# A random-feature attention and two expert layers on one core: wider VectorE and ScalarE steps, another share for GpSimd, token forms earlier

## The chip, the cores and the metric

The kernel runs on one core of one Trainium2 chip. What counts is device time in microseconds. The kernel before takes 965.62 us, the median of three runs (962.77 to 966.36).

## The reference

Three layers follow one another. The first is linear attention with random features, the others are two dense layers with a hidden width of 2048. Inputs are q, k, v of 4 x 8 x 576 x 64, 128 random features, and the weights, which come as 64-bit floats.

```python
def phi(x):                                  # random features, scaled by D ** -0.25
    proj = einsum('bhsd,md->bhsm', x, omega)
    h = proj - sum(x * x, -1) / 2
    return exp(h - max(h)) / sqrt(m)
q_p, k_p = phi(q_s), phi(k_s)
kv, z = einsum('bhsm,bhsd->bhmd', k_p, v), sum(k_p, axis=2)
x = (q_p @ kv) / (q_p @ z + 1e-6)            # 2304 tokens x 512
h = x @ w_in;   x = (h * cos(h)) @ w_out     # 512 -> 2048 -> 512
h = x @ w2_in;  x = (h * clip(h + 3, 0, 6) / 6) @ w2_out
```

## The kernel before, in words

**A planner writes the order.** Each piece of work is a task with a key (a due time), the engines that may do it with a duration for each, the tasks that it comes after, and the buffers that it takes and uses (`Plan.add`). `Plan.order` plays all tasks through: an engine that is free takes the ready task with the lowest key, if a slot of its buffer ring is free. Keys are formulas of tuned constants plus a tuned offset for each kind (`BIAS`). The result is the order of instructions on every engine. Where a task may go to VectorE or GpSimd, `SLOW` gives its durations and `ENGS` the choice, for each phase: 0 is the first two weight pairs and the first stop, 1 the rest of the first dense layer, 2 the second.

**Attention.** 18 chunks of 128 tokens, first the keys, then the queries (some of the queries among the keys). For each: a load, a projection, squares, a minimum on VectorE, the exponential on ScalarE, and matmuls. A query chunk ends in a transpose (line 626) and a copy into `xx`, the activations that stay in SBUF.

**Two splits.** Weights arrive as pairs of 32-bit words. `weight` makes 32-bit floats from them in one ScalarE step (line 698) and four VectorE steps (clamp line 702, shift 706, sign 712, low word 718), 512 columns at a time. Matmul operands are then split in a high part (rounded, `rnd`, line 377) and a low part (`sub`, line 384), and each product is three matmuls: high by high, low by high, high by low.

**First dense layer, four of 16 blocks of 128 hidden columns.** `pair_slot` computes them in the plain way (lines 827 and 853) beside the queries; this part I call the plain stage.

**The other 12 blocks, and all 16 of the second layer.** They go in pairs by a scheme of Strassen's kind: seven products (line 1062) replace eight. `pair_forms` makes seven weight forms of a pair (sums and differences, split), `forms` makes seven token forms `xf` of 768 tokens (b11, b21, b22, t1 to t4; four of them sums, line 1026) and stores them in DRAM (line 1041), from where later sweeps load them (line 994). A tour of 21 stops goes over seven sweeps of two pairs and three token ranges; each stop has two groups (`quad`), 42 groups in all. In a group the seven products go into four PSUM banks, which are seeded from one another by ScalarE (line 1075). VectorE adds for two of the four blocks (lines 1097 and 1100), and the nonlinear function follows for each block by itself: for cos lines 1127 or 1129, 1132, 1136 to 1141, 1145 or 1147, for the second layer lines 1114 and 1117; then the split into `g2`. One stop later `units` multiplies these by the second weight matrix (line 1186) into one of two banks, and line 1207 adds the bank to `xx`.

**Buffers.** `RINGS` names slots of shared memory. Weights arrive in `ws` and `ws2` and are converted in `wt` (three slots). `R2` lies on the memory of attention's buffers and opens when the last chunk is done (`open`).

All DMAs are issued from one queue, SP's, in the planner's order. Gaps of TensorE that the planner expects in attention are filled with small matmuls (lines 1252 and 1261).

Of the kernel before, what the change touches and what calls it, by code (L numbers as in the profile page):

```python
# [41 lines left out]
T_K = 5.034  # L42
T_Q = 18.765
T_S = 5.44
W_K0 = 32.072
W_KD = 0.874
W_AFTER = [3, 9]
W_F = [(-155.9, 30), (-90.9, 30)]
NS = 384
NP = 2 * NS  # L50
SWEEP = 2
L_PAIRS = [(NF - NG) // 2, NF // 2]
# [10 lines left out]
def stacked(space, at, *sizes):  # L63
    made = {}
    for ring, width, n in sizes:
# [9 lines left out]
    **stacked(F1, XX, ("ws", 1024, 3), ("wt", 512, 3), ("wk", 512, 3), ("yp", 512, 3)),  # L75
# [21 lines left out]
BIAS = {"sqnk": -64.1, "rd": 40.4, "kvs": 1.3, "g": 103.5, "xh": 39.3, "r1": 35.1, "gl": 52.5, "kv": -38.6, "b1q": 28.2, "h": 30.0, "in": -85.5, "W11": 34.6, "yp": -349.2, "xTk": -14.9, "y": 31.8, "vk": -12.4, "gh": 328.6, "tp": -94.6, "pjk": -188.3, "natk": -162.5, "xt": -131.2, "ek": -384.4, "sqq": 94.1, "xn": -159.4, "b1k": -156.9, "mxk": -366.5, "num": -75.3, "xl": 40.2, "sqnq": 187.5, "qt": -39.1, "xx": -230.5, "xTq": -5.7, "wk": -42.0, "natq": -168.8, "sn": -5.8, "W10": 92.9, "mxq": -40.0, "pjq": -166.6, "eq": -64.2, "sqk": -242.2, "out": 45.6, "ps": -16.5, "P00": 15.3, "P01": 37.0, "P10": 104.7, "P11": -4.2, "P20": -192.8, "P21": -393.2, "b2k": 16.5, "b2q": -82.4, "ba0": 35.7, "ba1": 81.9, "ba2": 86.8, "bb0": -448.0, "bb1": 142.2, "bb2": 367.5, "bc0": 84.4, "bc1": -169.0, "bc2": -161.9, "bd0": -180.6, "bd1": -359.0, "bd2": -149.6, "be0": -200.1, "be1": 38.4, "be2": -35.0, "c120": -131.9, "c121": 126.3, "c122": 262.4, "c220": -170.7, "c221": 104.1, "c222": -1.5, "consts": 162.6, "ev20": -93.6, "ev21": 76.5, "ev22": 130.6, "g20": -83.4, "g21": -262.0, "g22": 220.0, "gg0": 221.0, "gg1": -217.3, "gg2": -33.0, "gl20": -133.0, "gl21": 166.0, "gl22": 339.0, "ident": 199.0, "nq0": 283.2, "nq1": -8.6, "nr0": -36.2, "nr1": -65.2, "nt0": 119.2, "nt1": -3.2, "om": 115.1, "omr": -243.4, "open": -425.0, "pr0": -275.8, "pr1": -17.8, "pr2": -14.3, "pr3": 14.6, "psk": 147.5, "psq": -199.4, "rec": -225.8, "s50": 215.0, "s51": 54.7, "s52": -370.4, "sp0": -53.6, "sp1": -1.6, "sp2": -25.1, "st0": 54.8, "st1": -19.4, "st2": 54.1, "sum0": 103.2, "sum1": 208.3, "sum2": 101.9, "ta0": 37.4, "ta1": -8.1, "ta2": -7.3, "table": 15.7, "tb0": 37.6, "tb1": -7.2, "tb2": -1.3, "warm": 324.8, "wf0": 95.1, "wf1": 394.2, "wf2": -44.6, "wfh0": -163.2, "wfh1": -81.9, "wfh2": 218.8, "wfl0": 7.6, "wfl1": -44.7, "wfl2": -221.9, "wk20": -156.7, "wk21": -94.1, "wk22": -423.0, "wo0": -59.4, "wo1": -163.1, "wo2": 86.0, "woh0": -465.7, "woh1": -431.0, "woh2": -193.4, "wol0": 245.8, "wol1": 5.3, "wol2": -181.0, "xf0": 27.0, "xf1": 199.3, "xf2": 171.0, "xfl0": 210.5, "xfl1": 0.5, "xfl2": 234.6, "xst0": -135.9, "xst1": -249.1, "xst2": -136.0, "y20": -27.0, "y21": 31.9, "y22": 101.5, "yp21": -296.7, "yst": 9.8}  # L97
# [9 lines left out]
SLOW = {"sum": {"v": 0.42, "p": 0.89}, "wfla": {"v": 0.68, "p": 1.36}, "wflb": {"v": 0.42, "p": 0.89}, "wflc": {"v": 1.22, "p": 2.35}, "wol": {"v": 0.68, "p": 1.36},  # L107
        "gl2": {"v": 0.58, "p": 1.13}, "xfl": {"v": 0.95, "p": 1.83}, "ta": {"v": 0.95, "p": 1.83}, "xf": {"a": 0.84, "p": 1.3}}
ENGS = {"sum0": "v", "sum1": "v", "sum2": "p", "wfla0": "p", "wfla1": "p", "wfla2": "v", "wflb0": "p", "wflb1": "v", "wflb2": "v", "wflc0": "p", "wflc1": "p", "wflc2": "p", "wol0": "p", "wol1": "p", "wol2": "v", "gl20": "p", "gl21": "p", "gl22": "p", "xfl0b11": "v", "xfl0b21": "p", "xfl0b22": "v", "xfl1b11": "p", "xfl1b21": "p", "xfl1b22": "p", "xfl2b11": "p", "xfl2b21": "p", "xfl2b22": "v", "u0b": "a", "u1b": "a", "u0d": "a", "u1d": "a", "u0r": "v", "u1r": "v", "u0q": "v", "u1q": "v", "xfl0t1": "v", "xfl0t2": "v", "xfl0t3": "v", "xfl0t4": "p", "xfl1t1": "v", "xfl1t2": "v", "xfl1t3": "v", "xfl1t4": "v", "xfl2t1": "p", "xfl2t2": "p", "xfl2t3": "p", "xfl2t4": "p", "ta0t1": "p", "ta0t2": "v", "ta0t3": "p", "ta0t4": "v", "ta1t1": "p", "ta1t2": "v", "ta1t3": "p", "ta1t4": "v", "ta2t1": "v", "ta2t2": "v", "ta2t3": "v", "ta2t4": "p", "xf0": "ap", "xf1": "ap", "xf2": "a"}
# [50 lines left out]
class Plan:  # L160
# [9 lines left out]
    def order(self):  # L170
# [68 lines left out]
        while len(done) < len(tasks):  # L239
# [6 lines left out]
            while again:  # L246
                again = False
                for e in engines:
# [3 lines left out]
                    while pool[e]:  # L252
# [4 lines left out]
                        c = can(t, now)  # L257
# [19 lines left out]
                    free[e] = end  # L277
                    wake(end)
# [24 lines left out]
def attention_moe_moe2_kernel(  # L303
# [8 lines left out]
    eye: bass.AP,  # L312
    w1: bass.AP,
# [8 lines left out]
    halfpi, three, magic = (consts_[:, i:i + 1] for i in range(3))  # L322
# [45 lines left out]
    def wh(f):  # L368
        return held(plan.slot["wh", 1, f, 0], [128, 1024])

    def wl(f):
        sp, lo, hi = plan.slot["wh", 1, f, 0]
        return held((sp, lo + 1024, hi), [128, 1024])
# [25 lines left out]
    def consts(e):  # L399
        nc.gpsimd.memset(halfpi, HALFPI)  # L400
        nc.scalar.activation(out=junk, in_=halfpi, func=ACTF.Exp)
        nc.gpsimd.memset(three, 3.0)
        nc.gpsimd.memset(magic, MAGIC)
# [280 lines left out]
    def weight(src, m, f, hf, j=None):  # L684
        W = (m, f, hf)
        k = W_K0 + W_KD * (2 * f + hf) if j is None else w_key(j) + 6.0 * (f % 2) + 12.0 * hf
        cols = slice(512 * hf, 512 * hf + 512)

        def load(e):
            t = tile_of(("ws",) + W, [128, 1024], U32)  # L690
            nc.sync.dma_start(out=t, in_=src[f, :, 1024 * hf:1024 * hf + 1024])

        gate = [] if j is None else [("ba", 3 * j - 5 - j % 2)] if j >= SWEEP else [("in", W_AFTER[j], 3)]
        add(("ws",) + W, k - 8, {"d": 1.5}, load, gate + ([last_w[0]] if last_w[0] and j is None else []), alloc="ws" if j is None else "ws2", soft=[last_w[0]] if last_w[0] and j is not None else [])

        def mag(e):
            w = tile_of(("wt",) + W, [128, 512])
            nc.scalar.activation(out=w, in_=word(W, 1).bitcast(F32), func=ACTF.Abs)

        def clamp(e):  # L700
            w = buf[("wt",) + W]
            (nc.gpsimd if e == "p" else nc.vector).tensor_scalar(out=w, in0=w, scalar1=F64_HUGE, scalar2=F64_TINY, op0=ALU.min, op1=ALU.max)  # L702

        def shift(e):
            u = buf[("wt",) + W].bitcast(U32)
# [4 lines left out]
        def sign(e):  # L710
            u = buf[("wt",) + W].bitcast(U32)
# [4 lines left out]
        def low(e):  # L716
            u = buf[("wt",) + W].bitcast(U32)
# [4 lines left out]
        S_, T_ = ("ws",) + W, ("wt",) + W  # L722
# [608 lines left out]
```

## Time and profile before

| | |
|---|---|
| Median of three runs | 965.62 us |
| The profiled execution | 964.89 us, its span 963.0 us |
| TensorE busy (matmul) | 920.2 us, 96% |
| VectorE busy | 697.6 us, 72% |
| ScalarE busy | 562.5 us, 58% |
| GpSimd busy | 425.7 us, 44% |
| Mean granted clock of TensorE | 0.987 |

Attention runs from 0 to 220 us and the plain stage from 84 to 274 us. The groups of the first layer begin at 230 us, the last product ends at 930 us, the last matmul at 959 us. A busy share counts the time in which an engine has an instruction in work. A time of VectorE or GpSimd holds whatever the instruction waits for once it has begun.

### The profile page before, as it was taken

The page shows a single profiled execution, that of the slowest core. Times are in us where ns is not written, and L with a number is a line of the kernel's source. Part 1 is how long each engine was busy: PE and PEld are TensorE (multiplying, and loading weights), DVE is VectorE, ACT ScalarE, POOL GpSimd, SP SyncE. Part 2 cuts the span into 40 slices and gives each one's busy share as a digit, 9 for nine tenths or more (in the row PEclk, how much of TensorE's full clock was granted, in tenths as well). Part 3 has the DMA queues.
Part 4 walks back from the last instruction along what each step waited for, and adds up shares of the span by engine and source line. Part 5 has one row for each costly group of instructions (what it writes and reads, how often), then busy time and mean ns, then how long its engine had stood idle before and what let it go on. Part 6 is the DMA issues. An engine that isn't in the chain of part 4 may idle for free. (4 is left out here: it accounts for less than half of the span.)

```text
span 963.0 us, 18009 instructions
## 1 busy us (share of the span) xinstructions
PE 920.2 (96%) x6974; PEld 893.2 (93%) x6974; DVE 697.6 (72%) x1172; ACT 562.5 (58%) x1211; POOL 425.7 (44%) x342
## 2 busy tenths in 40 slices
PE   9999999999888999999998799999998999899998
PEld 8888999999888989989998699889998999899998
DVE  5896888767899996996799978763596459734332
ACT  7888787875655746646555666565463445334330
POOL 3431434215876443542455785761454135522230
PEclk9999999999999999999999999999999999999999
DMA  8754343213656539723561572354471257023512
GB/s 265 243 192 147 112 136 111 88 54 123 241 197 240 190 112 346 265 67 114 209 216 75 189 283 104 129 204 158 182 251 44 103 205 265 18 98 150 213 66 99
DMA packets 48134, 156.57 MB, mean 163 GB/s; under 512 B 4912, under 2 KB 16176, under 8 KB 48048
## 3 DMA queue, kind: packets, MB, share of 16 engines
q1 hardware_dynamic: 48048, 155.41, 45.6%
q8 instruction: 55, 0.90, 0.4%
q14 instruction: 31, 0.25, 0.1%
HBM read 112.93 MB, written 42.47 MB: 161 GB/s over the span
## 5 line engine op out<-in xcount | busy, mean ns | idle before, releaser
L384 POOL TENSOR_TENSOR R<-F,R 128x384 fp32r<-128x384 f32 (+3 forms) x254 | 336.9, 1345 | 420.9 <-ACT R L377 301.4
L377 ACT ACTIVATE R<-F 128x384 fp32r<-128x384 f32 (+4 forms) x306 | 173.9, 603 | 124.5 <-PE b L1186 40.6
L1186 PE MATMUL b<-R 128*128 128x384 f32 x1116 | 232.4, 338 | 10.3 <-DVE F L1207 10.1
L1186 PEld LDWEIGHTS b<-R 128*128 128x128 f32 x1116 | 198.7, 190 | 12.9 <-DVE F L1207 12.9
L1186 PE MATMUL b<-R,R 128*128 128x384 f32 x900 | 195.8, 339 | 8.0 <-DVE F L1207 7.9
L1062 PE MATMUL b<-R,R 128*128 128x384 f32 x978 | 187.7, 338 | 15.3 <-ACT b L1075 11.9
L1062 PEld LDWEIGHTS b<-R,R 128*128 128x128 f32 x978 | 171.8, 190 | 19.1 <-ACT b L1075 14.8
L1186 PEld LDWEIGHTS b<-R,R 128*128 128x128 f32 x900 | 161.6, 191 | 10.0 <-DVE F L1207 9.9
L1062 PE MATMUL b<-R 128*128 128x384 f32 x786 | 151.1, 339 | 1.5 <-ACT b L1075 1.5
L1207 DVE SCALAR_TENSOR_TENSOR F<-b,F 128x384 f32<-128x384 f32 x144 | 78.9, 552 | 93.5 <-PE b L1186 91.7
L1062 PEld LDWEIGHTS b<-R 128*128 128x128 f32 x786 | 140.0, 191 | 2.2 <-ACT b L1075 2.2
L1075 ACT ACTIVATE b<-b 128x384 f32<-128x384 f32 x126 | 60.0, 477 | 74.6 <-PE b L1062 73.2
L533 ACT ACTIVATE F<-b,F 128x128 f32<-128x128 f32 x288 | 81.6, 398 | 14.1 <-DVE F L518 12.8
L384 DVE TENSOR_TENSOR R<-F,R 128x512 fp32r<-128x512 f32 (+2 forms) x70 | 77.7, 1115 | 10.4 <-ACT R L377 7.9
L377 ACT ACTIVATE F<-b 128x512 f32<-128x512 f32 (+2 forms) x104 | 54.6, 540 | 30.4 <-PE b L1062 16.2
L507 DVE TENSOR_REDUCE F<-b 128x4 f32<-128x512 f32 x72 | 48.2, 684 | 22.2 <-PE b L490 14.1
L718 DVE SCALAR_TENSOR_TENSOR F<-F 128x512 uint32<-128x512 uint32 x64 | 62.7, 980 | 0.2
L853 PE MATMUL b<-R 128*128 128x256 f32 x432 | 60.0, 289 | 1.1 <-ACT F L869 1.1
L827 PE MATMUL b<-R 128*128 128x256 f32 x432 | 57.9, 286 | 0.3 <-DVE F L514 0.3
L712 DVE SCALAR_TENSOR_TENSOR F<-F 128x512 uint32<-128x512 uint32 x64 | 56.7, 886 | 0.6
L853 PEld LDWEIGHTS b<-R 128*128 128x128 f32 x432 | 54.9, 192 | 2.4 <-ACT F L869 1.3
L827 PEld LDWEIGHTS b<-R 128*128 128x128 f32 x432 | 53.8, 191 | 1.0 <-issue 0.5
(72 smaller groups left out, 1044.3 us busy)
## 6 DMA issues: line engine op xcount, KB each, us to landing
R<-xd SPq DMA_DIRECT2D x70, 768.0 KB, 7.0
F<-w SPq DMA_DIRECT2D x64, 512.0 KB, 4.4
xd<-R SPq DMA_DIRECT2D x42, 768.0 KB, 3.4
F<-vn SPq DMA_DIRECT2D x18, 260.0 KB, 4.5
F<-qT SPq DMA_DIRECT2D x18, 256.0 KB, 2.7
yy<-F SPq DMA_DIRECT2D x18, 256.0 KB, 2.3
F<-yy SPq DMA_DIRECT2D x24, 192.0 KB, 2.6
yT<-F SPq DMA_DIRECT2D x12, 384.0 KB, 2.4
```

The source lines that it names most:

```text
L377: nc.scalar.activation(out=o, in_=i, func=ACTF.Copy)
L384: (nc.gpsimd if e == "p" else nc.vector).tensor_tensor(out=o, in0=a, in1=b, op=ALU.subtract)
L507: nc.vector.tensor_reduce(out=buf[MX][:, o:o + 4], in_=pj, axis=AX.X, op=ALU.min)
L533: nc.scalar.activation(out=p[:, o], in_=pj[:, o], func=ACTF.Exp, scale=-1.0, bias=mx[:, b:b + 1])
L712: nc.vector.scalar_tensor_tensor(out=u, in0=word(W, 1), scalar=SIGN_HI, in1=u, op0=ALU.bitwise_and, op1=ALU.bitwise_or)
L718: nc.vector.scalar_tensor_tensor(out=u, in0=word(W, 0), scalar=29, in1=u, op0=ALU.logical_shift_right, op1=ALU.bitwise_or)
L827: nc.tensor.matmul(out=o, lhsT=w[:, 128 * kc:128 * kc + 128], rhs=v, start=(kc == 0 and j == 0), stop=(kc == KC - 1 and j == 2), skip_grou ...
L853: nc.tensor.matmul(out=y, lhsT=w[:, o], rhs=v, start=(first and fi == 0 and j == 0 and ec % 2 == 0), stop=(last and fi == 1 and j == 2 and ...
L1062: nc.tensor.matmul(out=o, lhsT=a, rhs=v, start=first and kc == 0 and q == 0, stop=kc == 1 and q == 2, skip_group_check=True)
L1075: nc.scalar.activation(out=buf[to][:, 0:NS], in_=buf[frm][:, 0:NS], func=ACTF.Copy)
L1186: nc.tensor.matmul(out=o, lhsT=a, rhs=v, start=q == 0, stop=q == 6 * SWEEP - 1)
L1207: nc.vector.scalar_tensor_tensor(out=o, in0=y, scalar=r, in1=o if s else buf[YP], op0=ALU.mult, op1=ALU.add)
```

## The change

- **Weights.** One staging slot of 2048 words (`ws2`), one conversion slot of 1024 columns (`wt`); `ws` has two slots of 2048. `weight` works on 1024 columns. The host packs each pair so that the front half holds the four blocks of the first matrix in the order in which forms need them, the rear half the second matrix. Splits of 512 and 256 columns become one of 768, two of 512 one of 1024.
- **Nonlinear function.** The two off-diagonal blocks lie side by side in `hs` and are done in one step of 768 columns (block "r"), also in their split; the diagonal ones ("b", "d") as before. Rings `g3` and `wk3` hold the wide tiles.
- **GpSimd.** `ENGS` chooses anew. The planner lets a GpSimd task and a VectorE task that reads only SBUF (`shares`) not overlap: both take a lock. The lock is the planner's; the kernel has no wait for it.
- **ScalarE.** Constants pi/2, 3 and the rounding constant are given as numbers, not as a column of a tile.
- **First stop's token forms.** With `AHEAD = 1` the seven forms of the first 768 tokens are made through one slot (`xe`) and two for sums (`te`) from key 150 on, stored in DRAM, and loaded when `R2` opens.
- **Order.** New keys and offsets throughout. A weight pair of each layer's second sweep waits for the last token form of that layer (`gate`). The seeds of a group come after the last seed of the group before. `SEED`, a list for another way to start output banks, is empty.

```diff
+AHEAD = 1
+AHEAD_AT = [150.0, 190.0, 220.0]
+AHEAD_BY = 4.0
+SEED = [[], [], [], [], [], [], []]
...
-    **stacked(F1, XX, ("ws", 1024, 3), ("wt", 512, 3), ("wk", 512, 3), ("yp", 512, 3)),
+    **stacked(F1, XX, ("ws", 2048, 2), ("wt", 1024, 1), ("wk", 512, 3), ("yp", 512, 2)),
...
-    "g2": spread(R1, 16384, 768, 8) + spread(R2, 13312, 768, 4),
-    "ws2": spread(F1, XX, 1024, 2),
-    "ta": spread(F1, XX + 1024, 768, 2),
+    "g2": spread(R1, 16384, 768, 4) + spread(R2, 13312, 768, 2),
+    "g3": spread(R1, 19456, 1536, 2) + spread(R2, 14848, 1536, 1),
+    "xe": spread(R1, 14336, 1536, 1),
+    "te": spread(F1, XX + 3072, 768, 1) + spread(F1, XX + 2048, 768, 1),
+    "ws2": spread(F1, XX, 2048, 1),
+    "ta": spread(F1, XX, 768, 2),
...
+SHARED = ("clamp", "shift", "sign", "low", "wl", "xl", "gl", "wfl", "wol", "st", "sum", "ta", "tb", "xfl", "gl2")
...
+            if (e == "p" or e == "v" and t.shares) and lock[0] > now:
+                return lock[0]
...
+                    if e == "p" or e == "v" and t.shares:
+                        lock[0] = end
...
-            w = tile_of(("wt",) + W, [128, 512])
-            nc.scalar.activation(out=w, in_=word(W, 1).bitcast(F32), func=ACTF.Abs)
+            nc.scalar.activation(out=tile_of(T_, [128, 1024]), in_=word(W, 1).bitcast(F32), func=ACTF.Abs)
...
+        gate = [("ba", 3 * j - 5 - j % 2)] if j >= SWEEP else [("in", W_AFTER[j], 3)]
+        for m in range(2):
+            if j == m * L_PAIRS[0] + SWEEP + 1:
+                gate.append(("tb", m, NT // NP - 1, "t4"))
...
-            nc.scalar.activation(out=buf[WK], in_=buf[WK], func=ACTF.Sin, scale=-TURN, bias=halfpi)
+            nc.scalar.activation(out=buf[WK], in_=buf[WK], func=ACTF.Sin, scale=-TURN, bias=HALFPI)
...
-        made = part("a", 0, 512, lambda: buf[f0], [f0], [low[0]], alloc="wf")
-        made += part("b", 512, 256, lambda: buf[f1][:, 256:512], [f1], [low[1]])
+        made = split("a", WF, FORM_HI, 0, 768, lambda: buf[T0][:, 0:768], [T0], [("low", j, 0)], 0, "wf")
...
+            ahead = s == 0 and p < AHEAD
+            if s not in heads or ahead:
...
+                    add(X, k + 2.0 * i - 14, {"d": 2.4}, load, [("xst", m, p, i)] + (["open"] if ahead else []), alloc="xf", soft=behind(i))
...
-            for r, c, h, done, dk in ((0, 0, A, c11, 5.2), (1, 1, ("c22", n), ("c22", n), 10.5), (0, 1, ("s5", n), ("c12", n), 12.1), (1, 0, Dk, c21, 13.8)):
+            for x, h, done, dk in (("b", A, c11, 5.2), ("r", HS, ("c12", n), 12.1), ("d", Dk, c21, 13.8)):
+                N = NP if x == "r" else NS
...
-                        nc.scalar.activation(out=tile_of(WK, [128, NS]), in_=buf[h][:, 0:NS], func=ACTF.Relu, bias=three)
+                        nc.scalar.activation(out=tile_of(WK, [128, N]), in_=hv(), func=ACTF.Relu, bias=3.0)
```

## Rows read from the trace of the kernel before

**Rows 1.** The page: busy us of each engine, share of the span, instructions.
```profile
PE 920.2 (96%) x6974; PEld 893.2 (93%) x6974; DVE 697.6 (72%) x1172; ACT 562.5 (58%) x1211; POOL 425.7 (44%) x342
```

**Rows 2.** Stretches: length, busy us of PE, PEld, DVE, ACT, POOL, clock, DMA.
```profile
150.00:205.00 55.00, 55.00 (x616) 51.79 (x617) 43.93 (x105) 45.01 (x100) 17.32 (x15) 1.00 0.30 97
...
230.00:330.00 100.00, 89.58 (x525) 87.44 (x525) 91.07 (x122) 63.19 (x124) 71.27 (x48) 0.95 0.60 218
330.00:430.00 100.00, 95.29 (x543) 93.69 (x542) 89.68 (x159) 58.43 (x114) 44.48 (x35) 1.00 0.58 200
...
500.00:555.00 55.00, 45.34 (x241) 43.74 (x240) 50.71 (x64) 29.85 (x58) 36.17 (x27) 0.95 0.42 158
555.00:650.00 95.00, 90.75 (x513) 89.02 (x512) 70.99 (x93) 57.93 (x113) 65.99 (x47) 0.99 0.48 176
650.00:830.00 180.00, 172.99 (x972) 171.07 (x971) 119.50 (x182) 87.51 (x173) 74.41 (x64) 0.98 0.45 164
830.00:959.00 129.00, 128.88 (x744) 128.56 (x742) 46.62 (x85) 41.66 (x84) 28.40 (x28) 1.00 0.31 114
```

**Rows 3.** Waits of TensorE: for whom, us in total, times, longest us.
```profile
PE b L1186 <- DVE F L1207: 18.1, 11, 3.1
PE b L1062 <- ACT b L1075: 13.5, 12, 3.4
```

**Rows 4.** Timeline 699 to 728 us: start, us, what, idle before.
```profile
705.78 0.41 DVE L702 TENSOR_SCALAR F<-F 128x512 f32<-128x512 f32 x1
...
708.59 0.68 DVE L718 SCALAR_TENSOR_TENSOR F<-F 128x512 uint32<-128x512 uint32 x1
...
720.85 1.22 DVE L712 SCALAR_TENSOR_TENSOR F<-F 128x512 uint32<-128x512 uint32 x1
721.49 3.99 POOL L384 TENSOR_TENSOR R<-F,R 128x384 fp32r<-128x384 f32 x3
...
723.14 1.48 DVE L718 SCALAR_TENSOR_TENSOR F<-F 128x512 uint32<-128x512 uint32 x1
...
725.61 0.79 PE L1186 MATMUL b<-R,R 128*128 128x384 f32 x3 [3.06 <-DVE F L1207]
```

**Rows 5.** Timeline 214 to 245 us.
```profile
219.25 0.60 PE L626 MATMUL b<-F 128*128 128x128 f32 x4
...
226.43 0.94 DVE L384 TENSOR_TENSOR R<-F,R 128x768 fp32r<-128x768 f32 x1
...
230.43 1.21 PE L1062 MATMUL b<-R 128*128 128x384 f32 x6
```

**Rows 6.** VectorE by line and shape: count, busy us, mean ns, idle before.
```profile
L718 DVE SCALAR_TENSOR_TENSOR F<-F 128x512 uint32<-128x512 uint32 x64 | 62.7, 980 | 0.2
L712 DVE SCALAR_TENSOR_TENSOR F<-F 128x512 uint32<-128x512 uint32 x64 | 56.7, 886 | 0.6
...
L702 DVE TENSOR_SCALAR F<-F 128x512 f32<-128x512 f32 x64 | 40.9, 638 | 10.4 <-ACT F L698 10.3
...
L1129 DVE TENSOR_SCALAR F<-F 128x384 f32<-128x384 f32 x36 | 28.0, 778 | 1.2
...
L1147 DVE SCALAR_TENSOR_TENSOR F<-F 128x384 f32<-128x384 f32 x36 | 25.7, 720 | 1.3 <-ACT F L1138 1.3
```

**Rows 7.** GpSimd by line and shape.
```profile
L384 POOL TENSOR_TENSOR R<-F,R 128x384 fp32r<-128x384 f32 x168 | 188.4, 1139 | 296.8 <-ACT R L377 196.4 <-PE b L1186 50.0 <-DVE F L1207 24.6
```

**Rows 8.** ScalarE by line and shape.
```profile
L1114 ACT ACTIVATE F<-F,consts 128x384 f32<-128x384 f32 x48 | 29.6, 616 | 19.3 <-DVE F L1097 11.1 <-DVE F L1100 6.1 <-POOL R L384 1.1
...
L1136 ACT ACTIVATE F<-F 128x384 f32<-128x384 f32 x36 | 18.6, 517 | 9.1 <-DVE F L1132 8.7
```

**Rows 9.** DMA issues: count, KB each, median us to landing.
```profile
R<-xd SPq DMA_DIRECT2D x70, 768.0 KB, 7.0
F<-w SPq DMA_DIRECT2D x64, 512.0 KB, 4.4
```

**Rows 10.** TensorE's fillers by line and shape.
```profile
L1252 PE MATMUL b<-F 128*128 128x128 f32 x46 | 7.7, 293 | 0.0
```

More of the change, by code (lines that the diff above doesn't have):

```diff
@@ L256, in order @@
                             continue
-                        c = can(t, now)
+                        c = can(t, now, e)
                         if c == 0.0 and any(
@@ L321, in attention_moe_moe2_kernel @@
     consts_ = const.tile([128, 16], F32, name="consts")
-    halfpi, three, magic = (consts_[:, i:i + 1] for i in range(3))
+    one = consts_[:, 0:1]
     space = {
@@ L399, in consts @@
     def consts(e):
[L400 to L403, printed above, removed]
+        nc.gpsimd.memset(one, 1.0)
+        nc.scalar.activation(out=junk, in_=one, func=ACTF.Exp)
         nc.gpsimd.memset(half, 0.5 * SCALE * SCALE)
@@ L988, in forms @@
             m = int(s >= heads[1])
-            if s not in heads:
+            ahead = s == 0 and p < AHEAD
+            if s not in heads or ahead:
                 for i, x in enumerate(names):
@@ L994, in load @@
                         nc.sync.dma_start(out=tile_of(X, [128, 2 * NP]).bitcast(F32), in_=xd[n_p * m + p, i])
-                    add(X, k + 2.0 * i - 14, {"d": 2.4}, load, [("xst", m, p, i)], alloc="xf", soft=behind(i))
-                return
-            gate = [("ba", n - 2)] if n else []
+                    add(X, k + 2.0 * i - 14, {"d": 2.4}, load, [("xst", m, p, i)] + (["open"] if ahead else []), alloc="xf", soft=behind(i))
+                if not ahead:
+                    return
+            gate = [("ba", n - 2)] if n and not ahead else []
             ready = [("ev2", s - 1, p, u) for u in range(8)] if m else [("xx", c) for c in range(NP // 128 * p, NP // 128 * (p + 1))]
@@ L1065, in product @@
                 add(name, k + 2.1 * ORDER.index(i), {"t": 1.04}, fn,
-                    forms_made + ([("xfl", int(s >= heads[1]), p, x)] if s in heads else []) + list(after), alloc=alloc, use=[X, ("wf", j)] + ([] if alloc else [bank_of]) + list(use))
+                    forms_made + ([("xfl", int(s >= heads[1]), p, x)] if s in heads and (s or p >= AHEAD) else []) + list(after), alloc=alloc, use=[X, ("wf", j)] + ([] if alloc else [bank_of]) + list(use))
                 return name
@@ L1077, in seed @@
                 add(to, k + dk - 10, {"a": 0.5}, fn, after, alloc=ring, use=[frm])
[L1079 removed]
+            first = ["open"] if n == 0 else [("ba", n - 1)] + ([("bd", 0)] if n == 1 else [("bd", n - 2)] if n else []) + ([("y", N_A - 1, 2)] if n == 2 else [])
             product(0, A, True, first, ring)
[L1081 removed]
+            seed(Bk, A, 1.1, [A] + ([("bd", n - 1)] if n else [f"pr{i}" for i in range(4)]))
             product(4, E, True, [A], ring)
+            HS = ("hs", n)
             def s5(e):
[L1085 to L1087 removed]
+                rnd(e, tile_of(HS, [128, NP])[:, 0:NS], buf[E][:, 0:NS])
+            add(HS, k + 3.2 - 8, {"a": 0.5}, s5, [("c22", n - 2)] if n > 1 else [], alloc="hs", use=[E])
             c11 = product(1, A, False, [Bk, E])
@@ L1134, in sine, with rest @@
+                    def rest(e, hv=hv, WK=WK):
+                        nc.vector.scalar_tensor_tensor(out=buf[WK], in0=buf[WK], scalar=MAGIC, in1=hv(), op0=ALU.subtract, op1=ALU.subtract)
                     def sine(e, WK=WK, on_act=on_act):
```

351 lines of the change are left out of this document (174 added, 177 removed).

## The prediction

> **What bounds the kernel now.** I read the busy shares first: TensorE is busy for 920.2 of 963.0 us and VectorE for 697.6 [rows 1]. So TensorE is the engine to feed, but a mean over the whole span hides where it starves, and the table by stretches is the view to read next [rows 2]. There the reader is to compare TensorE's busy time with the length of each stretch, and VectorE's beside it. From 830 to 959 us TensorE works without a break: 744 matmuls in 128.88 us, 0.173 us each, and this pace is a floor, because the change leaves every matmul of the three computing stages as it is. Elsewhere TensorE is idle for 10.42 us (230 to 330), 4.71 (330 to 430), 9.66 (500 to 555), 4.25 (555 to 650) and 7.01 (650 to 830): 36.05 us together. In the three worst of these stretches VectorE is busy for 91%, 90% and 92%; from 830 to 959, where nothing is lost, for 36%. The granted clock is the second loss. Short spells at 1.2 GHz, all of them in or right behind stretches in which TensorE stood still, make the column read 0.95, 0.95, 0.99 and 0.98: 5.0 + 2.75 + 0.95 + 3.6 = 12.3 us of full-speed time. So 36.05 + 12.3 = 48.4 us lie open behind 230 us, and 964.89 - 48.4 = 916 is what would be left with none of it.
>
> The waits of TensorE say who is late [rows 3]: 18.1 us for line 1207 (VectorE moves a finished output bank into the residual; there are only two such banks) and 13.5 us for line 1075 (ScalarE seeds the next product bank). Neither step is long. They are late because their engine's queue is behind. The timeline around the longest one shows how [rows 4]: GpSimd runs three subtractions in a row for 3.99 us, and beside them VectorE's line 712 takes 1.22 us and line 718 1.48 us, where line 718 takes 0.68 alone. The output bank's move starts behind these and TensorE waits 3.06 us. VectorE lost about 0.54 + 0.80 us on the two steps shown, some 45% of that stall, to running beside GpSimd.
>
> **The change, part by part.** All sums are against the profiled execution: 964.89 us, a span of 963.0 and 1.9 around it; the median of the runs, 965.62, is 0.7 above it.
>
> *Weights twice as wide.* The 64 half-width conversions become 32. Their four VectorE rows sum to 62.7 + 56.7 + 40.9 + 40.7 = 201.0 us [rows 6] (the last, line 706, is of line 702's kind). Alone, line 718 took 0.68 us for 512 columns and line 702 0.41 [rows 4], and a subtraction 0.94 for 768 [rows 5]. So 256 columns of the first kind cost 0.26, their fixed part is 0.16, and 384, 256 and 1024 columns cost 0.55, 0.42 and 1.20. No row shows a step at 1024 columns: twice a half-width step is the upper end, the fixed part less the lower. Clamp and shift then take 0.66 to 0.82; I take 0.8, nearest to the row. A set of 1.20, 1.20, 0.8 and 0.8 costs 4.0, and 32 sets 128 us: 73 less. If the wide steps collide as the narrow ones do now, 201.0 less the fixed parts (64 x 4 halved, 0.16 each: 20) is 181, only 20 less.
>
> *The two off-diagonal blocks in one step of 768 columns.* In the first layer lines 1129, 1132 and 1147 take 28.0 + 25.2 + 25.7 = 78.9 us in 36 triples [rows 6] (line 1132, between the two shown, is of line 1147's kind); 18 triples of three steps of at most 0.94 are 51 us: 28 less. Against it, the wide tile starts only when both blocks are there, so one block's answer is later by some 2 us. That is covered: the tiles are read one stop of the tour later, two groups of seven products on.
>
> *Work moved from GpSimd to VectorE.* Of the low halves of the activations (168 on GpSimd, 1139 ns each [rows 7]), 4 + 48 steps of 384 columns and 16 + 24 of 768 go to VectorE: 52 x 0.55 + 40 x 0.94 = 66 us. Weight forms go from 12 + 24 steps of 256 and 512 columns to 6 of 768 and 24 of 1024, 13 us more; the sums of weights from 24 to 56, 13 us; the token forms add 10 steps of 768, 9 us. Together 101 us more on VectorE, and GpSimd keeps about 190 of its 425.7 us, counted in the same way. VectorE's total is then 697.6 - 73 - 28 + 101 = 698. The four weight rows hold 201.0 - 64 x 2.18 = 61 us of lengthening beside GpSimd; if as much of that stays as GpSimd keeps, 45%, 27 us come back, and the rows that I left as they are give up about as much. I take 690, between 650 and 740. So VectorE does not become light. What changes is that a step of 0.7 us stays at 0.7 more often when an output bank waits behind it.
>
> The lengthening stands in the rows. The Trainium skill (SBUF — State Buffer, section "Who interferes with whom") gives a rule for it: a VectorE instruction with two SBUF inputs and a GpSimd one that reads SBUF exclude each other for the whole instruction. By it a wide step shuts GpSimd out for longer, and each collision costs the later of the two the rest of the other; in the rows GpSimd's three steps took 3.99 us where three means are 3.42, so both sides pay, as the rule has it. What that would make of the time is the rival "only the head" below.
>
> *Constants as immediates on ScalarE.* Line 1114 with a constant tile takes 616 ns, line 1136, the same shape without it, 517 [rows 8]. Of 186 such instructions 144 remain after merging: 14 us of ScalarE, or none if an immediate is fetched like a tile. ScalarE is never the engine that is full behind 230 us, so I count it at nothing by itself; were it the last link of each of 42 groups it would be 4 us.
>
> *First pass's token forms beside the queries.* This takes seven roundings, seven subtractions and four sums out of the stretch from 221 to about 245 us and puts them beside the queries: at most 7 x 2 x 0.517 = 7 us on ScalarE [rows 8], 3 x 0.94 = 3 on VectorE and, at twice a 384-column step's 1139 ns at the most [rows 7], 8 x 2.28 = 18 on GpSimd. Between 150 and 205 us GpSimd is busy for 17.32 of 55 and VectorE for 43.93 [rows 2], so they fit. If that cover fails, TensorE is late there by up to 10 us, ScalarE's 7 and VectorE's 3 taken whole. SP issues seven more loads of 768 KB and these wait for the last attention chunk; each lands 7.0 us after its issue [rows 9]. TensorE's last transpose of a chunk began at 219.25 us and the first product at 230.43 [rows 5], so there is room for one landing, and the later loads follow while the other products and the last blocks of the plain stage run. In the stretch 230 to 330 VectorE loses some 6 of its 91.07 us and GpSimd about as much.
>
> *Shared and fewer buffers, one more order.* One 2048-word staging slot for weights where there were two of half the size, one conversion slot where there were three; the token sums lie on the staging slot. Where a conversion is on time this costs nothing; its price if not is the rival below. The seeds of a group now come behind the last seed of the group before; both are ScalarE's and in that order already: nothing.
>
> *Keys and biases of the planner.* Every queue is written in another order. No row prices that. In the attention stage fillers of 7.7 us stand for gaps that the old plan expected [rows 10]; these may go (-8) or grow (+8), and I take zero.
>
> **The sum.** 230 to 330: 10.4 + 5.0 lost; the forms leave and GpSimd's runs shorten; I keep 5: -10. 330 to 430: 4.7 to 2.5: -2. 500 to 555: there the second layer's token forms and weights still meet, and VectorE gets more of them; 12.4 to 7: -5.5. 555 to 830: 11.3 + 4.5 lost; 45% as in the stall of rows 4: -7. Together -24.5: 964.9 - 24.5 = 940.
>
> **Rivals.** *Everything goes that is open.* All VectorE bursts dissolve and with them the low clock: 916, or, with a few us left, 922. For it: 830 to 959 shows the pace without loss. Against it: VectorE stays at 690.
>
> *Only the head gains.* GpSimd's rest still meets the wide steps (181 us for the weights in place of 128), so the low halves that it keeps and the output banks behind VectorE's longer steps are late as now, or the immediates are fetched like tiles. Then only the token forms help: -10, 955.
>
> *The stalls are dealt anew.* VectorE near 700 us means that first-layer groups need about as much VectorE as before (85 to 90% of 330 to 430), and another order puts the same waits elsewhere: 963.
>
> *Slower: one conversion slot.* Front and rear half of a pair now go through one slot in series. Front: ScalarE 1, four steps 4.0, rounding and subtraction of 768 columns 1.8, four sums 1.7, rounding and subtraction of 1024 columns 2.2: 10.7. Rear: 1 + 4.0 + 2.2 = 7.2. A load of 512 KB lands in 4.4 us [rows 9], one of 1 MB in about 8.5, of which some 4 lie beside the splitting of the half before: 2 x 4. With handovers that is 27 us a pair, and a pair is needed every three groups, 3 x 729 / 42 = 52 us. So it fits by half in the middle of a layer. At the head of a layer the token sums use the same memory, and the second pair's conversion waits behind the last token form. If there only 30 of the 52 us are left and VectorE's queue doubles the chain to 52, products start 22 us late at each of the two heads: 940 + 44 = 984. It decides from the point where the chain takes more than about 40 us. For it: VectorE at 92% from 500 to 555. Against it: the present chain of three slots is not what TensorE waits for in rows 3.
>
> **Chances.** Forecast 940 (932 to 950): 0.45. All gone, 922: 0.13. Head only, 955: 0.13. Dealt anew, 963: 0.12. One slot, 984: 0.17. Below 960.8, faster by over 0.5% (about what a measurement of this kernel can tell): 0.45 + 0.13 + 0.13 and 0.02 of the dealt anew, 0.73. Within 0.5%: 0.10. Slower: 0.17. The range runs from 918 to 974: under it lies a sliver of "all gone", over it most of "one slot".
>
> **What would show it.** Right: GpSimd's busy time under 250 us, line 718's successor near 1.2 us, TensorE's idle time from 230 to 330 under 6 us, waits for the output-bank move and the seed under 18 us together, and at most four spells of low clock. Wrong: a mean of 1.8 us for the wide steps (collisions stay); TensorE waiting for weight forms or for staged weights (one slot); waits of the old size at new places (dealt anew); a first product that starts after 245 us, which would say that the seven loads replaced the computing that they removed.

## The result, and the profile after

The changed kernel takes 918.68 us (median of four runs, 917.15 to 920.37) where the kernel before took 964.19 on the same chip: a ratio of 0.9534, 95% interval 0.9493 to 0.9576. The forecast was 940, the range 918 to 974; the time lies 0.7 us inside its lower end, beside the rival "everything goes that is open" (916, or 922 with a few us left). With runs from 917.15 to 920.37 us, on which side of 918 the median fell was luck.

The busy shares and the same stretches as in [rows 1, 2], and one around the only spell of low clock before the last matmul (length, busy us of PE, PEld, DVE, ACT, POOL, clock, DMA share, GB/s):

```profile
PE 906.9 (99%) x6970; PEld 886.2 (97%) x6970; DVE 671.3 (73%) x1095; ACT 537.2 (59%) x1070; POOL 179.6 (20%) x130
...
25.00:29.00 4.00, 4.00 (x49) 3.71 (x45) 1.29 (x2) 2.70 (x10) 1.04 (x1) 0.57 0.69 267
...
150.00:205.00 55.00, 55.00 (x612) 51.05 (x611) 37.77 (x83) 43.48 (x91) 22.62 (x17) 1.00 0.36 122
...
230.00:330.00 100.00, 99.98 (x648) 99.78 (x647) 76.98 (x112) 66.31 (x119) 40.34 (x23) 1.00 0.66 239
330.00:430.00 100.00, 100.00 (x578) 100.00 (x578) 87.37 (x135) 58.74 (x102) 16.20 (x13) 1.00 0.53 191
...
500.00:555.00 55.00, 55.00 (x320) 55.00 (x319) 48.13 (x72) 30.91 (x54) 12.99 (x8) 1.00 0.34 134
555.00:650.00 95.00, 95.00 (x549) 94.85 (x549) 70.62 (x99) 57.69 (x100) 15.04 (x8) 1.00 0.48 181
650.00:830.00 180.00, 180.00 (x1040) 180.00 (x1039) 128.38 (x198) 81.04 (x139) 7.37 (x4) 1.00 0.48 182
830.00:914.00 84.00, 83.72 (x483) 83.39 (x482) 36.63 (x61) 23.31 (x42) 0.00 (x0) 1.00 0.31 117
```

Behind 230 us TensorE has not stood still: 0.3 us are missing in these rows where 36.05 were. The clock stays at 2.4 GHz there. VectorE fell from 91% to 77% in the stretch that lost most (230 to 330), but hardly in the next two: 90% to 87% from 330 to 430, 92% to 88% from 500 to 555. GpSimd changed most, above all behind 330 us.

The waits of TensorE (us in total, times, longest), all that the view lists. The bank moves and seeds of [rows 3] are gone:

```profile
PE b L567 <- ACT F L552: 3.7, 2, 2.2
PE b L418 <- DVE F L415: 1.2, 1, 1.2
PE b L645 <- DVE F L631: 1.1, 2, 0.6
PE b L500 <- ACT F L552: 0.6, 2, 0.4
PE b L843 <- DVE F L808: 0.2, 1, 0.2
```

A set of weight steps in the timeline, with no GpSimd instruction beside it, and the first product (compare [rows 4, 5]):

```profile
245.05 1.21 PE L1055 MATMUL b<-R 128*128 128x384 f32 x6
...
597.60 0.69 DVE L717 TENSOR_SCALAR F<-F 128x1024 f32<-128x1024 f32 x1
598.32 0.69 DVE L721 TENSOR_SCALAR F<-F 128x1024 uint32<-128x1024 uint32 x1
599.05 1.23 DVE L727 SCALAR_TENSOR_TENSOR F<-F 128x1024 uint32<-128x1024 uint32 x1
600.31 1.23 DVE L733 SCALAR_TENSOR_TENSOR F<-F 128x1024 uint32<-128x1024 uint32 x1
```

The groups that answer to [rows 6, 7 and 9] (count, busy us, mean ns, idle before):

```profile
L727 DVE SCALAR_TENSOR_TENSOR F<-F 128x1024 uint32<-128x1024 uint32 x32 | 41.2, 1288 | 0.4
L733 DVE SCALAR_TENSOR_TENSOR F<-F 128x1024 uint32<-128x1024 uint32 x32 | 39.6, 1237 | 0.1
...
L717 DVE TENSOR_SCALAR F<-F 128x1024 f32<-128x1024 f32 x32 | 25.4, 794 | 6.8 <-ACT F L713 6.6
...
L721 DVE TENSOR_SCALAR F<-F 128x1024 uint32<-128x1024 uint32 x32 | 22.9, 717 | 0.3
...
L405 POOL TENSOR_TENSOR R<-F,R 128x768 fp32r<-128x768 f32 x26 | 49.4, 1901 | 265.7 <-ACT R L398 255.7 <-PE b L1055 6.2 <-DVE F L799 3.5
L405 POOL TENSOR_TENSOR R<-F,R 128x384 fp32r<-128x384 f32 x32 | 39.2, 1225 | 180.3 <-ACT R L398 141.2 <-issue 39.1
...
F<-w SPq DMA_DIRECT2D x32, 1024.0 KB, 5.2
```

The four wide steps sum to 129.1 us, near the 122.9 us that 32 sets like the one at 597.60 would take (0.69 + 0.69 + 1.23 + 1.23 = 3.84 us).

### The profile page after: what moved, and what is told of

Read it like the earlier page. It is cut to its first block, busy times and chain, and to the rows that moved or that the text cites. A ratio compares the mean times of both kernels' runs of the same rounds, so it can differ in the third digit from the quotient of the medians.

```text
span 917.8 us, 17375 instructions
## 1 busy us (share of the span) xinstructions
PE 906.9 (99%) x6970; PEld 886.2 (97%) x6970; DVE 671.3 (73%) x1095; ACT 537.2 (59%) x1070; POOL 179.6 (20%) x130
## 4 chain that ended last, share of the span: by engine, by line
PE 96%; DVE 2%; ACT 1%; DMA 0%; issue 0%; SPq 0%; ACTq 0%; DVEq 0%
PE b L1193 38%; PE b L1055 33%; PE b L843 6%; PE b L869 6%; PE b L500 4%; PE b L610 2%; PE b L567 2%; PE b L597 2%; PE b L509 1%; PE b L645 1%; ACT F L552 1%; PE b L1269 1%; DVE F L727 1%; DMA F<-kT 0%; DVE F L526 0%
## 5 line engine op out<-in xcount | busy, mean ns | idle before, releaser
L405 POOL TENSOR_TENSOR R<-F,R 128x384 fp32r<-128x384 f32 (+3 forms) x84 | 132.7, 1582 | 520.3 <-ACT R L398 469.7
L398 ACT ACTIVATE R<-F 128x768 fp32r<-128x768 f32 (+3 forms) x239 | 170.7, 736 | 67.9 <-PE b L1193 26.1
L1193 PE MATMUL b<-R,R 128*128 128x384 f32 x1080 | 204.8, 334 | 0.0
L1193 PEld LDWEIGHTS b<-R,R 128*128 128x128 f32 x1080 | 188.8, 188 | 0.0
L1055 PE MATMUL b<-R,R 128*128 128x384 f32 x954 | 182.8, 335 | 0.0
L1193 PE MATMUL b<-R 128*128 128x384 f32 x936 | 179.0, 334 | 0.0
L1055 PEld LDWEIGHTS b<-R,R 128*128 128x128 f32 x954 | 166.5, 188 | 0.4 <-ACT b L1068 0.2
L1193 PEld LDWEIGHTS b<-R 128*128 128x128 f32 x936 | 163.7, 188 | 0.0
L1055 PE MATMUL b<-R 128*128 128x384 f32 x810 | 155.6, 334 | 0.0
L405 DVE TENSOR_TENSOR R<-F,R 128x768 fp32r<-128x768 f32 (+3 forms) x166 | 142.7, 878 | 16.0 <-ACT R L398 14.8
L1055 PEld LDWEIGHTS b<-R 128*128 128x128 f32 x810 | 141.6, 188 | 0.0
L1220 DVE SCALAR_TENSOR_TENSOR F<-b,F 128x384 f32<-128x384 f32 x132 | 73.4, 556 | 72.8 <-PE b L1193 71.9
L843 PEld LDWEIGHTS b<-R 128*128 128x128 f32 x432 | 54.3, 191 | 1.6 <-issue 0.4
L869 PEld LDWEIGHTS b<-R 128*128 128x128 f32 x432 | 54.3, 191 | 0.9
L500 PE MATMUL b<-F 64*128 64x128 f32 x576 | 43.6, 287 | 0.7 <-ACT F L552 0.6
L1112 ACT ACTIVATE F<-b 128x384 f32<-128x384 f32 x48 | 23.4, 488 | 34.0 <-PE b L1055 32.3
```

Of the source, the lines that this page charges most:

```text
L398: nc.scalar.activation(out=o, in_=i, func=ACTF.Copy)
L405: (nc.gpsimd if e == "p" else nc.vector).tensor_tensor(out=o, in0=a, in1=b, op=ALU.subtract)
L500: nc.tensor.matmul(out=buf["pj", kind, c, o][:, 128 * i:128 * i + 128], lhsT=buf[X][64 * o:64 * o + 64, 128 * i:128 * i + 128], rhs=omd[64 ...
L843: nc.tensor.matmul(out=o, lhsT=w[:, 128 * kc:128 * kc + 128], rhs=v, start=(kc == 0 and j == 0), stop=(kc == KC - 1 and j == 2), skip_grou ...
L869: nc.tensor.matmul(out=y, lhsT=w[:, o], rhs=v, start=(first and fi == 0 and j == 0 and ec % 2 == 0), stop=(last and fi == 1 and j == 2 and ...
L1055: nc.tensor.matmul(out=o, lhsT=a, rhs=v, start=first and kc == 0 and q == 0, stop=kc == 1 and q == 2, skip_group_check=True)
```

## The experiments

Three theories stood against one another. *Collisions*: GpSimd's steps stretch VectorE's, and that alone made the old order late. *Order*: the new order puts bank moves and seeds in better places. *Load*: VectorE simply had too much to do, and width, immediates or the early forms took it away. Times are medians; the ratio to the kernel before on the same chip stands with its interval. The changed kernel's own is 0.9534 [0.9493, 0.9576].

### The old order without GpSimd's reads: before_no_reads and before_one_column

These decide what made the old order late. The edit is in `sub` of the kernel before, where the plan gave it to GpSimd; in the first run only zeros are written, three times; in the second:

```diff
+        if e == "p":
+            n = (slice(None),) * (len(o.shape) - 1) + (slice(0, 1),)
+            nc.gpsimd.tensor_tensor(out=o[n], in0=a[n], in1=b[n], op=ALU.subtract)
+            for _ in range(2):
+                nc.gpsimd.memset(o.bitcast(F32), 0.0)
+            return
```

Both leave out the low halves that GpSimd made, so they measure and are no kernels to use. GpSimd's sums and squares still read in both, although the first expectation counts the sums among what is left out.

> The kernel before, its order kept, but GpSimd's subtractions (low halves, sums) left out: in place of each GpSimd writes zeros to the same place three times, so that it is about as busy but reads nothing. Theory of collisions (two-sided: VectorE steps are stretched by GpSimd's reads, and that alone makes the old order late): the means of lines 702, 706, 712, 718 fall from 0.64-0.98 to 0.42-0.68 us, VectorE from 698 to 560-600 us, TensorE's waits from 38 to under 10 us, 918 to 930 us. Rival, theory of order (the old order puts bank moves behind bursts of weight steps, stretched or not): waits of 20 us or more stay, 945 to 960.

> The kernel before, its order kept. Each GpSimd subtraction is left out but for one column, which keeps its wait for the rounding by ScalarE; two writes of zeros behind it keep GpSimd about as busy as before. It tells apart what the run without reads changed at once: the reads beside VectorE, and the waits of GpSimd's queue. Theory of collisions: 912 to 922 us again, TensorE's waits under 10 us. Rival (the gain came from low halves that were early, because nothing waited for the rounding): 940 to 962.

Measured: 914.20 us, ratio 0.9477 [0.9458, 0.9497], and 910.64 us, ratio 0.9446 [0.9431, 0.9460], both under the ranges that the theory of collisions gave. The second keeps the waits of GpSimd's queue (301 us of them for the rounding) and nearly its busy time: for 384 columns its three steps take 0.27 + 2 x 0.43 = 1.13 us where the subtraction took 1.14. Its page, stretches, waits of TensorE, weight steps and GpSimd's steps:

```profile
PE 900.6 (99%) x6974; PEld 882.1 (97%) x6974; DVE 601.8 (66%) x1172; ACT 563.4 (62%) x1211; POOL 406.2 (45%) x850
...
230.00:330.00 100.00, 99.38 (x618) 99.02 (x617) 86.59 (x156) 72.42 (x142) 72.41 (x139) 1.00 0.67 236
330.00:430.00 100.00, 100.00 (x579) 100.00 (x578) 73.39 (x150) 60.65 (x122) 41.41 (x101) 1.00 0.54 193
...
500.00:555.00 55.00, 55.00 (x319) 55.00 (x318) 37.95 (x63) 37.35 (x71) 42.04 (x80) 1.00 0.67 248
...
PE b L1192 <- DVE F L1213: 0.7, 2, 0.3
PE b L1068 <- ACT b L1081: 0.6, 1, 0.6
...
L724 DVE SCALAR_TENSOR_TENSOR F<-F 128x512 uint32<-128x512 uint32 x64 | 46.8, 732 | 0.2
L718 DVE SCALAR_TENSOR_TENSOR F<-F 128x512 uint32<-128x512 uint32 x64 | 46.4, 725 | 0.5
L712 DVE TENSOR_SCALAR F<-F 128x512 uint32<-128x512 uint32 x64 | 33.7, 526 | 0.8
L708 DVE TENSOR_SCALAR F<-F 128x512 f32<-128x512 f32 x64 | 32.8, 513 | 14.0 <-ACT F L704 13.3
...
L388 POOL MEMSET R<- 128x384 f32 x336 | 144.8, 431 | 19.6
L386 POOL TENSOR_TENSOR R<-F,R 128x1 fp32r<-128x1 f32 x228 | 61.5, 270 | 354.5 <-ACT R L377 301.1 <-DVE F L1213 23.6 <-DVE F L724 15.6
```

Collisions hold for the old order. With the old order, old widths, constants as tiles and token forms made in the transition, TensorE's 18.1 + 13.5 us of waits shrink to 0.7 + 0.6, and the time falls by more than the change brought. VectorE lost 697.6 - 601.8 = 96 us of stretching. The rival (early low halves) falls, since the second kernel's low halves wait for the rounding and take about as long as before. Zeros as operands do not shorten a matmul: 579 in 100 us from 330 to 430, 0.173 us each, as in the kernel before.

### Parts alone in the old order: before_off_gpsimd, before_low_on_vector, before_immediates

```diff
-        (nc.gpsimd if e == "p" else nc.vector).tensor_tensor(out=o, in0=a, in1=b, op=ALU.subtract)
+        nc.vector.tensor_tensor(out=o, in0=a, in1=b, op=ALU.subtract)
```

> The kernel before, its order kept, with every subtraction of a split on VectorE; GpSimd keeps squares, roundings and sums, about 90 us. VectorE gets some 155 us and loses nearly all stretching: 698 + 155 - 115 = 740 us. Theory of collisions alone: 920 to 935. Rival, load: VectorE full from 230 to 430 us, TensorE waits 30 us there, 950 to 970.

Measured: 932.33 us, 0.9668 [0.9650, 0.9686]. For `before_low_on_vector` only the activations' low halves (`glo`) are issued so.

> The kernel before, its order kept, but the 168 low halves of the dense layers' activations issued on VectorE: one part of the change alone, with no new plan. VectorE gets 168 x 0.55 = 92 us, and loses the stretching by these steps, about 45% of some 125: 698 + 92 - 56 = 735 us; GpSimd 426 to 235. Theory that fewer collisions are worth more than the load: TensorE's waits fall from 36 to 15-20 us, 935 to 945. Rival, VectorE's load in the first dense layer (90% busy there already): no better than 960.

Measured: 948.45 us, 0.9837 [0.9817, 0.9856]; between the two theories' numbers. The page and worst stretch of each, `before_off_gpsimd` first:

```profile
PE 908.4 (98%) x6974; PEld 884.0 (95%) x6974; DVE 730.0 (78%) x1426; ACT 563.6 (61%) x1211; POOL 92.3 (10%) x88
...
230.00:330.00 100.00, 92.38 (x563) 89.91 (x562) 96.15 (x170) 66.51 (x129) 15.86 (x9) 0.98 0.63 228
```

```profile
PE 913.4 (97%) x6974; PEld 887.5 (94%) x6974; DVE 725.0 (77%) x1340; ACT 562.5 (60%) x1211; POOL 237.3 (25%) x174
...
230.00:330.00 100.00, 90.56 (x537) 87.92 (x536) 95.41 (x148) 64.33 (x126) 46.14 (x28) 0.97 0.62 224
```

Both have more VectorE time than the kernel before and are faster. So taking GpSimd away pays although VectorE gets its work, about two thirds of the change in one line; what is left stands where VectorE is at 95 to 96% (230 to 330 us), which fits the theory of load and was not tested by itself. The low halves are also done sooner on VectorE (570 ns for 384 columns, 1139 on GpSimd), and these two runs cannot set that apart.

```diff
-        nc.scalar.activation(out=buf[WK], in_=buf[WK], func=ACTF.Sin, scale=-TURN, bias=halfpi)
+        nc.scalar.activation(out=buf[WK], in_=buf[WK], func=ACTF.Sin, scale=-TURN, bias=HALFPI)
```

> The kernel before with its order, only the constants of ScalarE given as immediates: 186 instructions at some 0.10 us less, ScalarE 562 to about 545 us. Counted at nothing: within 4 us of the kernel before. Rival, that ScalarE's links stand in the chain of each group: 8 to 12 us less.

Measured, with all four places changed: 965.19 us, 1.0013 [0.9995, 1.0031]. The step itself became shorter, to 525 ns where [rows 8] have 616, and no gain came of it:

```profile
L1114 ACT ACTIVATE F<-F 128x384 f32<-128x384 f32 x48 | 25.2, 525 | 24.7 <-DVE F L1097 11.6 <-DVE F L1100 10.2 <-POOL R L384 1.4
```

### GpSimd's work put back in the new order: low_on_gpsimd and after_all_gpsimd

```diff
-                    sub(e, buf[G][:, N:2 * N], buf[WK], buf[G][:, 0:N].bitcast(F32))
+                    sub("p", buf[G][:, N:2 * N], buf[WK], buf[G][:, 0:N].bitcast(F32))
```

> The changed kernel with its order kept, but the low halves of the dense layers' activations (92 steps that it gives to VectorE) issued on GpSimd, as all 168 were before. VectorE has about 66 us less work of its own, GpSimd some 150 more (180 to about 320). Theory of collisions (GpSimd's runs stretch VectorE's steps and so delay what waits behind them): the wide weight steps go from 1.24-1.29 us to 1.5 or more, TensorE waits 10 to 20 us behind 230 us, the granted clock falls again in some spells, 930 to 945 us. Rival, theory of order (what counts is the new order, in which bank moves and seeds stand early): with VectorE lighter it stays at 918, within 4 us.

Measured: 917.83 us, 0.9514 [0.9479, 0.9548]: no change.

```profile
PE 907.0 (99%) x6970; PEld 886.2 (97%) x6970; DVE 637.5 (70%) x1003; ACT 537.0 (59%) x1070; POOL 322.6 (35%) x222
```

The clamp grew from 794 to 965 ns and the shift from 717 to 900, the two-input steps only from 1288 to 1338 and 1237 to 1248. The 92 steps that left VectorE held some 69 us and its busy time fell by 33.8, so some 35 us of stretching came back and cost nothing: here the theory of collisions missed. `after_all_gpsimd` does the same in the weight forms, the token forms and the sums of weights too; 18 subtractions of 512 columns and 15 token sums stay on VectorE.

> The changed kernel in its order, with the low halves of activations, weight forms and token forms and the sums of weights all issued on GpSimd: about 495 us there by the rows of the changed kernel (180 now, 426 before), VectorE some 150 lighter. Theory of collisions: as many steps are stretched as before, TensorE waits 20 us or more behind 230 us, 940 to 970 us. Rival, the new order is wide enough to bear it: 917 to 926.

Measured: 933.74 us, 0.9678 [0.9661, 0.9696], between the two theories' numbers. Its page, first stretch and waits:

```profile
PE 911.6 (98%) x6970; PEld 885.8 (95%) x6970; DVE 588.3 (63%) x891; ACT 537.1 (58%) x1070; POOL 476.2 (51%) x334
...
230.00:330.00 100.00, 94.09 (x602) 92.19 (x602) 60.97 (x79) 60.09 (x109) 76.91 (x47) 1.00 0.64 233
...
PE b L1055 <- POOL R L405: 4.5, 7, 1.1
PE b L1055 <- ACT b L1068: 3.4, 4, 1.1
...
PE b L1193 <- DVE F L1220: 2.1, 2, 1.7
```

The 204 steps that left VectorE held 156.6 us and its busy time fell by 83.0: some 74 us of stretching came back. With that, and with more GpSimd time than the kernel before, the new kernel loses 15 us and not 45, and the largest wait behind 230 us in total is GpSimd's own lateness. So it bears collisions without loss up to a point between 323 and 476 us of GpSimd, and beyond it is still 30 us faster than the kernel before. Taking the reads away is one way to the gain, then, and not the only one. What makes the new kernel bear them, its order, its widths or a VectorE that is lighter by 109 us in this run (588.3 where it had 697.6), no run sets apart.

### The plan: no_lock, old_keys and late_forms

```diff
-            if (e == "p" or e == "v" and t.shares) and lock[0] > now:
-                return lock[0]
```

> The changed kernel planned without the lock that keeps GpSimd's tasks and VectorE's SBUF-only tasks from overlapping in the plan; keys, engines and sizes are kept. Theory of collisions: VectorE's busy time rises from 671 by 20 us or more, TensorE waits 5 to 15 us behind 230 us, 925 to 935. Rival (GpSimd's 180 us are few enough that it does not matter where they lie): within 4 us of 918.

Measured: 995.72 us, 1.0307 [1.0275, 1.0339]. Far outside both theories' numbers, and it does not decide between them: VectorE's busy time rose by 20 us, as the theory of collisions had it, but the largest wait is one of 19.7 us for a rounding by ScalarE. Without the lock the same offsets give another order:

```profile
586.40 1.06 ACT L396 ACTIVATE R<-F 128x1024 fp32r<-128x1024 f32 x1 [16.53 <-PE b L1191]
...
606.03 1.01 PE L1053 MATMUL b<-R 128*128 128x384 f32 x2 [19.67 <-ACT R L396]
```

A rounding of weights waits 16.5 us for second products, and behind it two halves of weights go through the one conversion slot in series, the steps of the first from 588.75 us, those of the second until 604.11, before the second layer's products start. This is the stall that the prediction described in its rival "one conversion slot" (22 us at a layer's head). It did not come in the changed kernel; whether it stays away hangs on the order.

`old_keys` replaces the offsets in `BIAS` by those of the kernel before where both have them.

> The changed kernel planned anew, with the offsets of the kernel before for every kind of task that both know. Engines, widths, immediates, buffers and the planner's lock are the new ones. Theory of collisions: with GpSimd at 180 us it stays under 930. Theory of order (the offsets that were found for this plan carry the gain): TensorE waits 20 to 50 us, 940 to 970.

Measured: 943.63 us, 0.9778 [0.9759, 0.9796]. With VectorE at 668.8 us and GpSimd at 172.2, about as in the changed kernel, 25 us are lost by the order; the number is that of the theory of order. So few collisions are not enough, and the new plan needs offsets of its own (this run also has 50 more filler matmuls). The kernel before had an order that works as soon as its steps are not stretched (910.64 us).

```diff
-AHEAD_AT = [150.0, 190.0, 220.0]
-AHEAD_BY = 4.0
+AHEAD_AT = [280.0, 320.0, 350.0]
+AHEAD_BY = 1.1
```

> The changed kernel planned anew with the keys of the first stop's token forms moved from 150-174 to 280-287, so that they come at the end of the queries and not beside them. Theory that the early forms clear the transition: the first product starts 5 to 10 us later or TensorE waits as much between 205 and 300 us, 923 to 928 us. Rival, that the transition was cleared by the missing collisions alone: within 3 us of 918.

Measured: 917.47 us, 0.9505 [0.9479, 0.9532]. The edit moved nothing: the seven stores of these forms began between 118.8 and 184.1 us, in the changed kernel between 117.5 and 184.7. The planner gave the tasks to engines that were free early, whatever their key. The run says nothing about the early forms. The runs without reads do: there the forms were made in the transition, and TensorE lost 0.6 and 1.2 us between 230 and 330.

### Width and fillers: halves and after_no_fillers

```diff
-            nc.vector.scalar_tensor_tensor(
-                out=u, in0=word(W, 1), scalar=SIGN_HI, in1=u, op0=ALU.bitwise_and, op1=ALU.bitwise_or
-            )
+            for o in (0, 512):
+                nc.vector.scalar_tensor_tensor(
+                    out=u[:, o:o + 512], in0=word(W, 1)[:, o:o + 512], scalar=SIGN_HI, in1=u[:, o:o + 512], op0=ALU.bitwise_and, op1=ALU.bitwise_or
+                )
...
```

> The changed kernel in its order, with VectorE's wide steps issued as two halves each: the four weight steps as 2 x 512 columns, the steps of the off-diagonal blocks' nonlinear function as 2 x 384. Some 200 more instructions at about 0.13 us: VectorE 671 to about 695. Theory that width frees VectorE: it was 87% busy from 330 to 430 us, so TensorE waits there and at 500 to 555, 922 to 930. Rival (VectorE has room as long as nothing stretches its steps): 918 to 920.

Measured: 919.22 us, 0.9521 [0.9494, 0.9549]: as the changed kernel. VectorE went from 671.3 to 685.1 us in 206 more instructions, 91% busy from 330 to 430 us, and TensorE still lost nothing there. So width by itself brought no gain that this can tell, in an order with few collisions. `after_no_fillers` leaves out the small matmuls that fill planned gaps in attention.

> The changed kernel without its 50 fillers in attention (8.2 us of TensorE). If they only stand in gaps: within 2 us of 918; if they push matmuls of the chunks: up to 6 us less; if without them the granted clock falls in the gaps: up to 5 us more. I expect no change.

Measured: 916.57 us, 0.9508 [0.9492, 0.9523]; the intervals overlap, so a gain of 2 us is not shown.

## Why the prediction was right, and where it was short

**What bounds the kernel** stood as said: the 36 us of idle time and the 12 us of low clock behind 230 us were the open sum, and the pace of 0.173 us was the floor. The balance of the spans, 963.0 - 917.8 = 45.2: idle time behind 230 us -35.8, low clock behind 230 us about -12, against it before 230 us 4.4 us more idle time (6.8 of 230 in place of 2.4; the exponentials, line 552 of the changed kernel, are awaited for 4.3 of it) and some 1.7 of low clock. The 3 us left I did not trace.

**The cause** stood for the old order: line 718's stretching beside GpSimd, shown in [rows 4], was read as the reason why short steps are late, and the runs without reads leave 1.2 + 0.9 and 0.7 + 0.6 us of these waits. It is not shown to be all that the change brought: with 74 us of stretching put back the new kernel keeps 30 of its 45 us. One reading in [rows 4] was off. The step of 0.68 us at 708.59 was not alone, for GpSimd began 0.05 us behind it; the price holds by the step at 716.88, beside an idle GpSimd:

```profile
708.64 3.45 POOL L384 TENSOR_TENSOR R<-F,R 128x384 fp32r<-128x384 f32 x3 [3.34 <-ACT R L377]
...
716.88 0.67 DVE L718 SCALAR_TENSOR_TENSOR F<-F 128x512 uint32<-128x512 uint32 x1
...
717.69 3.83 POOL L929 TENSOR_TENSOR F<-F 128x256 f32<-128x256 f32 x4 [2.56 <-DVE F L718]
```

**The step that failed is the sum:** 24.5 us were forecast to go and 45.5 went. I let 5 + 2.5 + 7 + 8.8 us stay, the last by the 45% of one stall and the others without a row. Measured, 0.3 us of idle time stayed, and none of the low clock. The 45% was too small already for the stall that it was read from: I counted the stretching of the two steps that stand last, but VectorE had worked without a gap since 713.2 us, and more of its steps were stretched:

```profile
714.15 1.27 DVE L706 TENSOR_SCALAR F<-F 128x512 uint32<-128x512 uint32 x1
...
717.81 1.09 DVE L1117 SCALAR_TENSOR_TENSOR F<-F 128x384 f32<-128x384 f32 x1
718.83 0.96 DVE L706 TENSOR_SCALAR F<-F 128x512 uint32<-128x512 uint32 x1
719.71 1.22 DVE L384 TENSOR_TENSOR R<-F,R 128x512 fp32r<-128x512 f32 x1
...
722.00 1.22 DVE L384 TENSOR_TENSOR R<-F,R 128x256 fp32r<-128x256 f32 x1
```

With the two of [rows 4] these are seven steps of 8.46 us together. At the shortest lengths of their shapes (0.41, 0.55, 0.41, 0.68, 0.68, 0.42 and 0.68) they would take 3.83. The 4.6 us between are more than the whole stall of 3.06. The rival "everything goes" got 0.13 with the argument that VectorE stays near 690 us. This was the wrong test: 671 us, at 87 to 88% in a stretch (91% in `halves`), hold no one up when the steps take about what the plan allows for them. The old plan gave clamp and sign 0.42 and 0.7 us in the dense layers' pairs and they took 0.64 and 0.89; the new one gives 0.75 and 1.25, and they take 0.79 and 1.29. The signs that I named for "right" all came (GpSimd 179.6 us, the low step 1.24, 0.02 us of idle time from 230 to 330, no wait for bank move or seed), but they would have come with this rival too, so they do not speak for the sum.

**By parts.** *Width*: the wide set came out at 129.1 us (128 counted), GpSimd at 179.6 (190), VectorE at 671.3 (690). As a saving of time, width cannot be told from nothing (`halves`: 919.22 us; its interval is about 5 us wide). *Off GpSimd*: alone worth 31 us in the old order (963.33 - 932.33); I had no term for it by itself. *Immediates*: 0, as counted. *Early forms*: I put most of the head's 10 us on them; nothing shows that they were needed. Their cover held. My sign against them, a first product after 245 us, came (245.05) and meant nothing: plain-stage matmuls stood before it. *One conversion slot*: loads of 1 MB landed in 5.2 us, not 8.5, and no wait for a weight form is listed; its stall came in `no_lock`.

**The Trainium skill's rule** (SBUF — State Buffer, "Who interferes with whom") says that a VectorE step with two SBUF inputs collides with GpSimd's reads and not with its writes, and that tensor_scalar in its two-port mode contends with GpSimd, without that distinction. The traces agree: beside GpSimd's writes of zeros in `before_one_column` the two-input steps took 0.73 us (0.67 alone, 0.89 and 0.98 before), clamp and shift 0.51 and 0.53 (0.41 alone, 0.64 before). Some sums and squares on GpSimd still read in that run, and that this tensor_scalar runs in the two-port mode no view shows.

## What to carry to other kernels

When an engine that feeds the bound one is late, compare each of its steps with the shortest instance of the same shape before counting its load: a mean 44% above it (0.98 us for 0.68), with another engine's instruction beside the long instances, was the finding here, and it was worth more than the steps' number or width. Price its removal by all stretched steps back to the last gap of that engine's queue, not by the last two before the stall. And if an order is written from assumed durations, put the collisions into the durations or keep the colliding engine off. The offsets found for one model of the engines did not carry over to another here (995.72 us without the lock, 943.63 with the old offsets).

## What the runs showed of the hardware that was not expected

GpSimd at 45 to 51% busy left TensorE's listed waits behind 230 us under 3 us when its subtractions were replaced by writes (VectorE 601.8 to 612.1 us; some 80 us of sums, squares and roundings stayed). The subtractions themselves, 337 of GpSimd's 426 us in the kernel before, cost 96 us of VectorE time.
